# A first channel product with 15 multiplications for 18 on the last five token groups

## Chip, cores, metric

The kernel runs on one core of one Trainium2 chip. The metric is the device time of the program in microseconds (us). The profile's span runs from the first to the last instruction; the time is a little longer than the span.

## What is computed

A delta-rule attention over 4 batches, 8 heads, 768 tokens and a head size of 48, in which a 48x48 state per head is updated token by token, is followed by a mixer: a low-rank mixing over the tokens, and a channel block with a ReLU between two products.

```python
for t in range(S):                                   # S = 768
    y[:, :, t] = einsum('bhd,bhde->bhe', q[:, :, t], state)
    v_old = einsum('bhde,bhd->bhe', state, kt)       # kt: normalised key
    state = state + bt * einsum('bhd,bhe->bhde', kt, vt - v_old)
x = y.transpose(0, 2, 1, 3).reshape(B, S, 384)
h = x.transpose(0, 2, 1) @ U @ V                     # rank 32
u = x + h.transpose(0, 2, 1)
out = u + maximum(u @ w_ch1, 0) @ w_ch2              # 384 -> 1536 -> 384
```

All of it is float32.

## The kernel before

**Units and batches.** Attention goes in eight units n (batch b = n // 2, half of the sequence n % 2). A unit is loaded into one of two SBUF areas, `slots[n % 2]`, so that unit n + 2 is loaded only when unit n's recurrence no longer needs its slot. Its steps are: transpositions and products of keys and queries (`turn`, `products`: L671, L698), a triangular substitution on VectorE (`blocks`: L774, L783, L789, L796), the joining of its blocks (`joins`: L879, L882, then after a copy L887 the products L897, L900), two preparing products (`prepare`: L1000, L1011), and then six steps of the recurrence (`recur`: L1049 computes `b`, L1062 subtracts it on VectorE, L1077 and L1089 update the state, L964 and L978 give the outputs).

**Token groups.** The mixer works on twelve groups of 256 tokens (b, i), three to a batch. `front` mixes the tokens (L1378 once per batch, L1398, the addition L1407) and transposes the result into `ut` (L1426, L1429). `channels` is the first channel product: six steps e, each a pair of output tiles of 128, each tile three matmuls of 256 columns (the contraction of 384 is three tiles of 128), and `relu` (L1452) follows. The pair can be done as full-array matmuls (L1487) or in quarters of 64x64 (L432), which spares a change of array mode beside attention's quarter matmuls. `narrow` is the second channel product, in seven half-size products for eight (a Strassen-like scheme over halves of contraction, tokens and outputs): seven times six matmuls of 192 columns (L1602), with sums of activations from `add_up` (L1514) and `last_sum` (L1521). `gather` (L1527) adds the results to X on VectorE, and SP stores.

**The last batch.** For the three groups of batch 3 the first product is already done another way: `first_of_last` runs `quick(f)` for six f over all 768 tokens, in eleven matmuls of 384 columns (L1282) for twelve. Its sums of weights (L1242, L1250) and of tokens (L1266) are made on VectorE, and partial results go through ScalarE copies (L1300, L1304, L1309) and VectorE additions from PSUM (L1291).

```python
mm(px, w1_of(f, 0), u(0, 0), start=True, stop=True)
mm(pz, n1, t1, start=True, stop=True)
mm(py, w1_of(f, 1), u(1, 0), start=True)
mm(py, w1_of(f, 2), u(2, 0), stop=True)
...
mm(px, w1_of(f + HF, 1), t4)
mm(px, w1_of(f + HF, 2), t5, stop=True)
```

**What sets the order.** The instruction streams are written by a planner inside the kernel's own Python. Each step is a generator that yields `need(...)` (events that must have been emitted) or `op(engine, cost, mode, take, give)`. `run` picks, among the steps that could start next, the one with the lowest place, using planned costs in us, and then emits its instructions. A table `PLACES` gives most steps a place by name. PSUM has eight banks; the planner hands them out as four pairs (`pair`) for attention and fronts, and as single banks (`mix`) for the channel products. `reserve` takes banks 6 and 7 from the pairs for `mix` when batch 0 is nearly through its recurrence.

Of the kernel before, what the change touches and what calls it, by code (L numbers as in the profile page):

```python
# [19 lines left out]
GT = 256  # L20
# [6 lines left out]
def kernel(  # L27
# [52 lines left out]
    BANK = dict(pair=[0, 2, 4, 6], mix=[6, 7])  # L80
# [9 lines left out]
    SWITCH, HOLD, STAY = 0.18, 0.18, 0.15  # L90
    LOT, FETCH = 256, 4.1
    SPAN, PHASE = 3.413, 2.0

# [49 lines left out]
    add_up b0 i0 31.18; add_up b0 i1 51.08; add_up b0 i2 92.4; add_up b1 i0 4.76; add_up b1 i1 120.37  # L143
    add_up b1 i2 37.32; add_up b2 i0 75.44; add_up b2 i1 84.89; add_up b2 i2 77.05; add_up b3 i0 118.73
    add_up b3 i1 13.96; add_up b3 i2 89.72; blocks n0 109.59; blocks n1 122.78; blocks n2 46.87; blocks n3 118.73
    blocks n4 113.47; blocks n5 111.09; blocks n6 106.05; blocks n7 118.23; both -17.1; channels b0 i0 e0 48.87
    channels b0 i0 e0 quad 1; channels b0 i0 e1 -24.59; channels b0 i0 e1 quad 1; channels b0 i0 e2 105.07
    channels b0 i0 e3 120.72; channels b0 i0 e4 93.87; channels b0 i0 e4 quad 1; channels b0 i0 e5 71.17
    channels b0 i0 e5 quad 1; channels b0 i1 e0 91.19; channels b0 i1 e1 29.66; channels b0 i1 e1 quad 1
    channels b0 i1 e2 105.84; channels b0 i1 e3 111.44; channels b0 i1 e4 29.68; channels b0 i1 e5 93.86  # L150
    channels b0 i1 e5 quad 1; channels b0 i2 e0 126.42; channels b0 i2 e1 -13.48; channels b0 i2 e1 quad 1
    channels b0 i2 e2 123.41; channels b0 i2 e2 quad 1; channels b0 i2 e3 110.59; channels b0 i2 e4 29
    channels b0 i2 e4 quad 1; channels b0 i2 e5 29; channels b0 i2 e5 quad 1; channels b1 i0 e0 121.9
    channels b1 i0 e1 45.62; channels b1 i0 e2 51.81; channels b1 i0 e3 119.36; channels b1 i0 e3 quad 1
    channels b1 i0 e4 91.86; channels b1 i0 e4 quad 1; channels b1 i0 e5 88.71; channels b1 i0 e5 quad 1
    channels b1 i1 e0 92.89; channels b1 i1 e0 quad 1; channels b1 i1 e1 0.3; channels b1 i1 e2 123.36
    channels b1 i1 e3 87.93; channels b1 i1 e3 quad 1; channels b1 i1 e4 93.42; channels b1 i1 e4 quad 1
    channels b1 i1 e5 2.19; channels b1 i2 e0 75.94; channels b1 i2 e0 quad 1; channels b1 i2 e1 50.31
    channels b1 i2 e2 89.43; channels b1 i2 e2 quad 1; channels b1 i2 e3 121.39; channels b1 i2 e4 35.38
    channels b1 i2 e4 quad 1; channels b1 i2 e5 37.37; channels b1 i2 e5 quad 1; channels b2 i0 e0 110.33  # L160
    channels b2 i0 e0 quad 1; channels b2 i0 e1 38.43; channels b2 i0 e1 quad 1; channels b2 i0 e2 103.35
    channels b2 i0 e3 106.45; channels b2 i0 e3 quad 1; channels b2 i0 e4 123.83; channels b2 i0 e5 74.54
    channels b2 i0 e5 quad 1; channels b2 i1 e0 54.8; channels b2 i1 e0 quad 1; channels b2 i1 e1 13.42
    channels b2 i1 e2 104.03; channels b2 i1 e2 quad 1; channels b2 i1 e3 20.9; channels b2 i1 e3 quad 1
    channels b2 i1 e4 63.86; channels b2 i1 e4 quad 1; channels b2 i1 e5 20.4; channels b2 i1 e5 quad 1
    channels b2 i2 e0 41.46; channels b2 i2 e0 quad 1; channels b2 i2 e1 106.94; channels b2 i2 e1 quad 1
    channels b2 i2 e2 87.46; channels b2 i2 e2 quad 1; channels b2 i2 e3 20.4; channels b2 i2 e3 quad 1
    channels b2 i2 e4 24.2; channels b2 i2 e4 quad 1; channels b2 i2 e5 36.8; channels b2 i2 e5 quad 1
    copies 112.79; cut 126.91; diagonals n0 h0 55.7; diagonals n0 h1 53.68; diagonals n1 h0 3.93
    diagonals n1 h1 92.39; diagonals n2 h0 104.44; diagonals n2 h1 11.15; diagonals n3 h0 61.76  # L170
    diagonals n3 h1 33.65; diagonals n4 h0 47.84; diagonals n4 h1 106.43; diagonals n5 h0 1.02
    diagonals n5 h1 21.33; diagonals n6 h0 109.11; diagonals n6 h1 116.22; diagonals n7 h0 93.85
    diagonals n7 h1 75.29; first 110.09; first_of_last 49.99; front b0 i0 108.02; front b0 i0 quad 1
    front b0 i1 84.31; front b0 i2 91.39; front b0 i2 quad 1; front b1 i0 -10.61; front b1 i1 112.1
    front b1 i2 110.61; front b1 i2 quad 1; front b2 i0 63.6; front b2 i0 quad 1; front b2 i1 7.31
    front b2 i2 122.28; front b3 i0 105.93; front b3 i1 20.22; front b3 i2 109.1; gather b0 i0 h0 c0 -8.96
    gather b0 i0 h0 c1 -24.09; gather b0 i0 h1 c0 118.73; gather b0 i0 h1 c1 120.73; gather b0 i1 h0 c0 111.61
    gather b0 i1 h0 c1 94.36; gather b0 i1 h1 c0 118.74; gather b0 i1 h1 c1 94.39; gather b0 i2 h0 c0 30.48
    gather b0 i2 h0 c1 107.43; gather b0 i2 h1 c0 111.47; gather b0 i2 h1 c1 111.47; gather b1 i0 h0 c0 6.76
    gather b1 i0 h0 c1 111.08; gather b1 i0 h1 c0 110.6; gather b1 i0 h1 c1 111.1; gather b1 i1 h0 c0 122.88  # L180
    gather b1 i1 h0 c1 0.79; gather b1 i1 h1 c0 94.35; gather b1 i1 h1 c1 123.23; gather b1 i2 h0 c0 89.9
    gather b1 i2 h0 c1 121.66; gather b1 i2 h1 c0 1.2; gather b1 i2 h1 c1 108.09; gather b2 i0 h0 c0 118.24
    gather b2 i0 h0 c1 30.64; gather b2 i0 h1 c0 116.23; gather b2 i0 h1 c1 87.96; gather b2 i1 h0 c0 124.29
    gather b2 i1 h0 c1 109.6; gather b2 i1 h1 c0 117.94; gather b2 i1 h1 c1 29.2; gather b2 i2 h0 c0 21.73
    gather b2 i2 h0 c1 -8.77; gather b2 i2 h1 c0 30.5; gather b2 i2 h1 c1 113.04; gather b3 i0 h0 c0 -15.09
    gather b3 i0 h0 c1 61.92; gather b3 i0 h1 c0 14.46; gather b3 i0 h1 c1 91.38; gather b3 i1 h0 c0 -17.58
    gather b3 i1 h0 c1 118.32; gather b3 i1 h1 c0 11.47; gather b3 i1 h1 c1 15.47; gather b3 i2 h0 c0 90.44
    gather b3 i2 h0 c1 -10.43; gather b3 i2 h1 c0 -5.75; gather b3 i2 h1 c1 18.02; grams n0 i0 34.54
    grams n0 i1 3.69; grams n1 i0 -9.32; grams n1 i1 11.14; grams n2 i0 30.14; grams n2 i1 108.59; grams n3 i0 -2.69
    grams n3 i1 141.92; grams n4 i0 47.78; grams n4 i1 8.96; grams n5 i0 70.76; grams n5 i1 37.82; grams n6 i0 31.98  # L190
    grams n6 i1 9.07; grams n7 i0 111.04; grams n7 i1 60.31; joins n0 h0 27.2; joins n0 h1 55.69; joins n1 h0 3.19
    joins n1 h1 66.38; joins n2 h0 57.15; joins n2 h1 91.87; joins n3 h0 92.39; joins n3 h1 34.88; joins n4 h0 92.36
    joins n4 h1 105.93; joins n5 h0 94.89; joins n5 h1 21.39; joins n6 h0 -5.16; joins n6 h1 1.19; joins n7 h0 66.85
    joins n7 h1 104.02; last_sum b0 i0 110.92; last_sum b0 i1 116.73; last_sum b0 i2 103.44; last_sum b1 i0 -18.95
    last_sum b1 i1 -19.07; last_sum b1 i2 38.32; last_sum b2 i0 116.24; last_sum b2 i1 85.38; last_sum b2 i2 19.73
    last_sum b3 i0 109.31; last_sum b3 i1 -17.59; last_sum b3 i2 109.9; load n0 namek halves(0,) -16.25
    load n0 namek halves(1,) 28.17; load n0 nameq halves(0,) 4.52; load n0 nameq halves(1,) 67.79
    load n0 namev halves(0,) 127.05; load n0 namev halves(1,) 113.04; load n0 namez halves(0,) 5.44
    load n0 namez halves(1,) 99.93; load n1 namek halves(0,) 5.43; load n1 namek halves(1,) 60.81
    load n1 nameq halves(0,) -16.24; load n1 nameq halves(1,) 118.91; load n1 namev halves(0,) 47.34  # L200
    load n1 namev halves(1,) 49.87; load n1 namez halves(0,) 64.38; load n1 namez halves(1,) -10.34
    load n2 namek halves(0, 1) 21.89; load n2 nameq halves(0, 1) 22.39; load n2 namev halves(0, 1) 148.73
    load n2 namez halves(0, 1) -23.39; load n3 namek halves(0, 1) 70.26; load n3 nameq halves(0, 1) 40.96
    load n3 namev halves(0, 1) 63.6; load n3 namez halves(0, 1) 38.96; load n4 namek halves(0, 1) 94.39
    load n4 nameq halves(0, 1) 109.61; load n4 namev halves(0, 1) 45.72; load n4 namez halves(0, 1) 92.39
    load n5 namek halves(0, 1) 123.32; load n5 nameq halves(0, 1) 10.48; load n5 namev halves(0, 1) 78.69
    load n5 namez halves(0, 1) 10.98; load n6 namek halves(0, 1) 95.9; load n6 nameq halves(0, 1) 93.9
# [1473 lines left out]
```

## Time and profile before

| | before |
|---|---|
| time, median of 3 runs | 613.3 us (612.89 to 614.26) |
| profiled execution: time | 611.88 us |
| profiled execution: span | 610.2 us |
| mean granted clock of TensorE | 0.941 |
| TensorE (PE) busy | 571.3 us, 94% |
| VectorE (DVE) busy | 417.4 us, 68% |
| ScalarE (ACT) busy | 237.1 us, 39% |

Busy is the time in which at least one instruction of the engine runs. PE is the matmuls and PEld the weight loads that go ahead of them. A line of the grouped view names the source line, the engine, the operation, the tiles written and read, the number of records, their busy time and the mean length of one. In the timeline, records of one kind that follow one another are merged: start, length from the first start to the last end, and count.

### The profile page before, as it was taken

The page shows a single profiled execution, that of the slowest core. Times are in us where ns is not written, and L with a number is a line of the kernel's source. Part 1 is how long each engine was busy: PE and PEld are TensorE (multiplying, and loading weights), DVE is VectorE, ACT ScalarE, POOL GpSimd, SP SyncE. Part 2 cuts the span into 40 slices and gives each one's busy share as a digit, 9 for nine tenths or more (in the row PEclk, how much of TensorE's full clock was granted, in tenths as well). Part 3 has the DMA queues.
Part 4 walks back from the last instruction along what each step waited for, and adds up shares of the span by engine and source line. Part 5 has one row for each costly group of instructions (what it writes and reads, how often), then busy time and mean ns, then how long its engine had stood idle before and what let it go on. Part 6 is the DMA issues. An engine that isn't in the chain of part 4 may idle for free.

```text
span 610.2 us, 25422 instructions
## 1 busy us (share of the span) xinstructions
PE 571.3 (94%) x11502; PEld 497.0 (81%) x11502; DVE 417.4 (68%) x1000; ACT 237.1 (39%) x478; POOL 98.4 (16%) x169
## 2 busy tenths in 40 slices
PE   4788886699999999999999999999999999999997
PEld 4677876578888988988989987988989878656997
DVE  4999897898998528898887388869852124332542
ACT  2756654445522552246225522373152231344000
POOL 9141051520004110411032104300010000000000
PEclk9976556799999999999999999999999999999999
DMA  9731677921004320620050025300000000000000
GB/s 140 127 81 56 209 177 152 219 46 56 3 28 70 51 49 3 99 67 3 15 98 17 22 48 91 63 17 4 16 14 2 30 3 1 26 1 0 19 34 27
DMA packets 63852, 33.39 MB, mean 55 GB/s; under 512 B 50816, under 2 KB 61824, under 8 KB 63744
## 3 DMA queue, kind: packets, MB, share of 16 engines
q1 hardware_dynamic: 56800, 23.21, 18.4%
q0 software_dynamic: 5344, 8.27, 6.6%
q8 instruction: 90, 1.47, 1.0%
q10 hardware_dynamic: 1600, 0.30, 0.3%
q14 instruction: 18, 0.15, 0.1%
HBM read 27.03 MB, written 4.72 MB: 52 GB/s over the span
## 4 chain that ended last, share of the span: by engine, by line
PE 82%; DVE 10%; ACT 3%; issue 3%; DMA 1%; ACTq 0%; DVEq 0%
PE P L1602 26%; PE P L1487 18%; PE P L432 8%; PE P L1282 7%; PE P L698 3%; PE P L671 2%; PE P L1049 2%; PE P L978 2%; PE P L1011 2%; PE P L1000 2%; PE P L964 2%; PE P L1077 1%; DVE xt L789 1%; DVE prod L783 1%; PE P L853 1%
## 5 line engine op out<-in xcount | busy, mean ns | idle before, releaser
L1487 PE MATMUL P<-ut,w_sb 128*128 128x256 f32 x480 | 111.4, 385 | 0.4
L1487 PEld LDWEIGHTS P<-ut,w_sb 128*128 128x128 f32 x480 | 88.9, 190 | 12.9 <-ACT hs L1452 1.1
L1602 PE MATMUL P<-w_sb,hs 128*128 128x192 f32 x492 | 87.2, 331 | 0.1
L1602 PEld LDWEIGHTS P<-w_sb,hs 128*128 128x128 f32 x492 | 79.5, 190 | 2.7 <-ACT hs L1452 0.8
L1527 DVE TENSOR_TENSOR X<-X,P 128x192 f32<-128x192 f32 x84 | 29.5, 351 | 60.9 <-PE P L1602 59.3
L789 DVE TENSOR_TENSOR xt<-xt,prod 128x112 f32<-128x112 f32 (+21 forms) x200 | 64.6, 323 | 6.9
L783 DVE TENSOR_TENSOR prod<-gs,xt 128x112 f32<-128x112 f32 (+21 forms) x200 | 64.0, 320 | 4.6
L1452 ACT ACTIVATE hs<-P 128x512 f32<-128x512 f32 x54 | 32.3, 598 | 86.9 <-PE P L1487 66.0
L1602 PE MATMUL P<-w_sb,S 128*128 128x192 f32 x288 | 49.7, 328 | 0.0
L1602 PEld LDWEIGHTS P<-w_sb,S 128*128 128x128 f32 x288 | 46.7, 190 | 0.4 <-issue 0.3
L432 PE MATMUL P<-ut,w_sb 64*64 64x256 f32 x672 | 45.1, 383 | 1.8 <-ACT ut L1429 0.9
L948 ACT COPY X<-P 64x192 f32<-64x192 f32 x96 | 30.0, 312 | 38.1 <-PE P L978 29.7
L671 PE MATMUL P<-ident,slot 128*128 128x128 f32 x180 | 29.5, 315 | 11.0 <-DMA slot<-in_k_dram 9.4
L918 ACT COPY slot<-zz 32x384 f32<-32x384 f32 x64 | 32.4, 508 | 13.6 <-DVE zz L796 8.1
L555 POOL DMA_DIRECT2D slot<-in_k_dram x44 | 29.0, 667 | 44.1 <-PE P L1077 44.0
L671 PEld LDWEIGHTS P<-ident,slot 128*128 128x128 f32 x180 | 24.4, 163 | 13.3 <-issue 9.8
L555 POOL DMA_DIRECT2D slot<-in_q_dram x32 | 21.0, 665 | 84.0 <-DVE wide L1242 33.7
L698 PE MATMUL P<-slot 48*64 48x64 f32 x1536 | 32.1, 236 | 2.5 <-ACT slot L685 1.9
L1282 PE MATMUL P<-slot,w_sb 128*128 128x384 f32 x96 | 33.3, 486 | 0.0
L698 PEld LDWEIGHTS P<-slot 48*64 48x64 f32 x1536 | 29.0, 149 | 5.3 <-ACT slot L685 2.6
L555 POOL DMA_DIRECT2D slot<-in_v_dram x32 | 21.2, 669 | 70.7 <-PE P L671 63.0
L685 ACT COPY slot<-P 128x768 f32<-128x768 f32 x30 | 23.6, 797 | 22.8 <-PE P L671 17.5
(152 smaller groups left out, 978.5 us busy)
## 6 DMA issues: line engine op xcount, KB each, us to landing
out_dram<-X SPq DMA_DIRECT2D x22, 192.0 KB, 1.9
X<-in_moe_w_ch_dram SPq DMA_DIRECT2D x10, 384.0 KB, 4.2
wide<-in_moe_w_ch_dram SPq DMA_DIRECT2D x10, 384.0 KB, 4.3
slot<-in_k_dram SPq DMA_DIRECT2D x48, 72.0 KB, 5.0
slot<-in_k_dram POOLq DMA_DIRECT2D x44, 72.0 KB, 5.1
slot<-in_q_dram SPq DMA_DIRECT2D x32, 72.0 KB, 5.0
slot<-in_q_dram POOLq DMA_DIRECT2D x32, 72.0 KB, 5.5
slot<-in_v_dram SPq DMA_DIRECT2D x32, 72.0 KB, 3.0
```

The source lines that it names most:

```text
L432: nc.tensor.matmul(to[half(g)], w[half(r), half(g)], x[half(r)], start=start, stop=stop, skip_group_check=True,)
L555: queue.dma_start(out=t[half(1 - g if name == "z" else g), :, to, 0:D], in_=src[b, 4 * g + s, hf * UC * L : (hf + 1) * UC * L, :].rearrang ...
L671: nc.tensor.transpose(p_t[:, c // 3, c % 3], t[:, c, 2 * j : 2 * j + 2].rearrange("p s d -> p (s d)"), ident,)
L698: nc.tensor.matmul(p_g[half(g ^ (par * i)), par, c], kq[rows, c, j, 0, half(g)], kq[rows, c, j, i, half(g)], start=True, stop=True,)
L783: nc.vector.tensor_tensor(out=prod, in0=gb[:, :, j : j + 1, j + 1 :].to_broadcast([128, split, m, w]), in1=xb[:, :, 0:m, j : j + 1].to_bro ...
L789: nc.vector.tensor_tensor(out=xb[:, :, 0:m, j + 1 :], in0=xb[:, :, 0:m, j + 1 :], in1=prod, op=ALU.subtract,)
L918: nc.scalar.copy(pg[quarter(i), :, at, :, a : a + BK], cut(zc, h)[quarter(i)].rearrange("p r (c j) t -> p r c j t", j=2),)
L948: nc.scalar.copy(x[half(c % 2), c // 2, 4 * D * g : 4 * D * (g + 1)].rearrange("p (j r d) -> p r j d", r=2, d=D), states(p_y)[half(g)],)
L1282: nc.tensor.matmul(to, w, t, start=start, stop=stop, skip_group_check=True)
L1452: nc.scalar.activation(hs[:, fs[0] : fs[1] + 1 : fs[1] - fs[0]], p_f, ACTF.Relu)
L1487: nc.tensor.matmul(p_f[:, x], w(x, t), ut[:, t], start=(t == 0), stop=(t == KT - 1))
L1602: nc.tensor.matmul(to, of[0], of[1], start=of[2], stop=of[3], skip_group_check=True)
```

## The change

The first product of the last five groups, (2, 1), (2, 2), (3, 0), (3, 1) and (3, 2), is done in fifteen products for eighteen. The outputs are cut in thirds (four tiles of 128), the contraction in thirds (one tile of 128), and a group's tokens in halves (128). Each of the fifteen products is a sum of weight blocks times a sum of token blocks: four matmuls of 128 columns into one PSUM bank. The products are arranged in five chains. Within a chain each product is accumulated onto the bank's running sum, and between two products the bank is read: ScalarE copies it to the activations or VectorE adds or subtracts it there (`drain`), sixteen times for a group, and a ReLU pass follows. Fourteen sums of weight blocks are made once, in `slots[0]`, and eleven sums of token blocks for each group. Activations and sums of every second of the five groups lie in `slots[1]`. The chains use four PSUM banks (0 to 3), which `reserve` takes from the pairs when batch 3 has computed its last `b` and its last outputs. `quick`, `first_of_last` and their sums go; batch 3's groups become ordinary groups of 256 tokens.

Together with it the pairs of output tiles are put together otherwise (`PAIRS`), each weight slice is converted by a step of its own, many planned costs of the planner are set anew (a few are shown), and the table `PLACES` is new throughout. In the diff, cut to its core and with `CHAINS` set in fewer lines, a product of a chain is given as its weight block, its token block and, for each output that the bank is read into, that output, the sign, and how many terms it has had before.

```diff
-    BANK = dict(pair=[0, 2, 4, 6], mix=[6, 7])
+    BANK = dict(pair=[0, 2, 4, 6], mix=[6, 7, 0, 1, 2, 3])
...
-    SWITCH, HOLD, STAY = 0.18, 0.18, 0.15
+    SWITCH, HOLD, STAY = 0.11, 0.18, 0.15
+    LAP = 0.085
...
-    PAIRS = ((0, 1), (2, 6), (7, 8), (3, 4), (5, 9), (10, 11))
+    PAIRS = ((0, 1), (6, 7), (2, 8), (3, 9), (4, 5), (10, 11))
...
-        for i in range(len(slices)):
+        def convert(i, last):
...
-            yield need(("wide", i))
+            yield need(("wide", i), ("weights", last))
...
+    LAST, EARLY = B - 1, 7
+    W_SUMS = (
+        (6, 1, 7, 1), (8, 1, 9, -1), (3, 1, 10, 1), (5, 1, 11, -1), (1, 1, 4, -1), (12, -1, 13, -1),
+        (0, -1, 10, -1), (3, -1, 9, 1), (3, 1, 6, -1), (4, 1, 12, -1), (2, -1, 14, -1), (13, -1, 16, -1),
+        (2, 1, 15, 1), (0, 1, 9, -1),
+    )
+    T_SUMS = (
+        (1, 1, 5, 1), (2, 1, 4, 1), (3, 1, 7, 1), (0, 1, 6, 1), (2, -1, 3, -1), (5, -1, 8, -1),
+        (1, 1, 3, -1), (6, 1, 7, 1), (0, -1, 2, 1), (0, -1, 1, -1), (4, 1, 9, 1),
+    )
+    CHAINS = (
+        ((0, 0, ((0, 1, 0),)), (15, 9, ((1, -1, 1),)), (22, 6, ((5, -1, 1),)),
+         (16, 13, ((3, -1, 3),)), (11, 16, ((2, 1, 2),)), (17, 14, ((4, 1, 0),))),
+        ((1, 3, ((1, 1, 0),)), (14, 8, ((3, 1, 1),)), (18, 10, ((2, -1, 1),)), (19, 4, ((0, -1, 1),))),
+        ((20, 7, ((2, 1, 0),)), (12, 11, ((3, -1, 2),))),
+        ((10, 15, ((3, 1, 0), (5, 1, 0))), (21, 5, ((1, 1, 2),))),
+        ((7, 12, ((5, -1, 2),)),),
+    )
+    CHAIN_BANKS, TERMS = (2, 3, 4, 5, 4), (2, 3, 3, 4, 1, 3)
+    def ordinal(b, i):
+        return NG * b + i - EARLY
...
     def weight_sums():
-        yield need(("weights", W2 + 5), ("narrow", 1, 0))
...
+        yield need(("weights", W2 - 1), *freed(N - 2))
+        for z, (a, s, c, t) in enumerate(W_SUMS):
+            yield op("dve", dve(512), port=True)
+            sum_of(w_block(9 + z), w_block(a), s, w_block(c), t)
+            emitted(("weight sum", 9 + z), 0.1)
...
+    def token_sums(b, i):
+        yield need(
+            ("front", b, i), *[("wide", *before(*before(b, i)))] * (ordinal(b, i) > 1),
+            *freed(N - 1 if ordinal(b, i) % 2 else N - 2),
+        )
+        for z, (a, s, c, t) in enumerate(T_SUMS):
+            yield op("dve", dve(128), port=True)
+            sum_of(token(b, i, 6 + z), token(b, i, a), s, token(b, i, c), t)
+            emitted(("token sum", b, i, 6 + z), 0.1)
...
+    def products_of(b, i, e):
+        y = CHAIN_BANKS[e]
+        yield need(
+            ("front", b, i), ("mixing", 0), *[("chain", b, i, x) for x in range(e) if CHAIN_BANKS[x] == y],
+            *[("chain", *before(b, i), x) for x in range(len(CHAINS)) if CHAIN_BANKS[x] == y and ordinal(b, i)],
+        )
+        bank = mixed(y).rearrange("p (q n) -> p q n", q=4)
+        def drain(c, outs, final):
+            yield need(cleared(b, i), *freed(N - 1) * (ordinal(b, i) % 2))
+            for z, (o, s, k) in enumerate(outs):
...
+                if k == 0:
+                    yield op("act", act(512), rush=True, give=give)
+                    nc.scalar.activation(
+                        to, p, ACTF.Relu if TERMS[o] == 1 else ACTF.Copy, scale=float(s)
+                    )
+                else:
+                    yield need(("held", b, i, o, k - 1))
+                    yield op("dve", dve(512), rush=True, give=give)
+                    nc.vector.tensor_tensor(
+                        out=to, in0=to, in1=p, op=ALU.add if s > 0 else ALU.subtract
+                    )
...
+        for c, (w, t, outs) in enumerate(CHAINS[e]):
+            yield need(
+                *[("drained", b, i, e, c - 1)] * (c > 0 and len(CHAINS[e][c - 1][2]) > 0),
+                *[("weight sum", w)] * (w > 8), *[("token sum", b, i, t)] * (t > 5),
+            )
+            yield op("pe", 0.875, "F", take=None if c else ("mix", y), words=16)
+            for q in range(4):
+                nc.tensor.matmul(
+                    bank[:, q], w_block(w)[:, q // 2, 128 * (q % 2) : 128 * (q % 2) + 128],
+                    token(b, i, t), start=c == 0 and q == 0, stop=True,
+                    skip_group_check=True,
+                )
...
-    def quick(f):
...
-    def first_of_last():
...
     def reserve():
...
+        yield need(("b", LAST, NC - 1))
+        yield op("pe", 0.0, take=("pair", 0))
+        free["mix"].update({2: state["now"], 3: state["now"]})
+        emitted(("mixing", 0))
+        yield need(*[("x", LAST, c) for c in range(NC)])
+        yield op("pe", 0.0, take=("pair", 1))
+        free["mix"].update({4: state["now"], 5: state["now"]})
...
     def wide(b, i):
-        yield need(("front", b, i), ("half" if b == LAST else "narrow", *before(b, i), *[3] * (b == LAST)))
+        yield need(("front", b, i), cleared(b, i), *freed(N - 1) * (ordinal(b, i) > 0 and ordinal(b, i) % 2))
...
-        if b == LAST:
+        if ordinal(b, i) >= 0:
             for f0 in range(0, HF, 3):
                 begin(add_up(f0, ()), 4)
...
         else:
             for e in range(len(PAIRS)):
                 begin(channels(e), 95)
...
-        begin(first_of_last(), 94)
...
+                if ordinal(b, i) >= 0:
+                    begin(first_of(b, i), 94)
```

## Prediction

> **What bounds the kernel now.** I read the page first, then the stage table (busy time of each engine in each stretch), then the timeline of TensorE for the price of one product, then the waits at the end. On the page, the slices tell the shape: the granted clock is low in the first fifth and full from about 122 us on, and from there PE is at nine tenths or more to the last slice.
>
> ```profile
> PE 571.3 (94%) x11502; PEld 497.0 (81%) x11502; DVE 417.4 (68%) x1000; ACT 237.1 (39%) x478; POOL 98.4 (16%) x169
> PE   4788886699999999999999999999999999999997
> DVE  4999897898998528898887388869852124332542
> PEclk9976556799999999999999999999999999999999
> ```
>
> The stage table says the same in us, cut at three events: the clock's rise, the end of the last substitution on VectorE (its transposition L796 starts at 445.9) and the start of the last batch's mixing (L1378 at 500.7).
>
> ```profile
> 0.00:122.00 122.00, 91.53 (x2706) 83.17 (x2710) 102.47 (x244) 64.82 (x125) 43.29 (x76) 0.71 0.72 145
> 122.00:446.00 324.00, 320.82 (x7100) 282.95 (x7093) 259.37 (x641) 129.38 (x260) 53.51 (x89) 1.00 0.20 42
> 446.00:500.00 54.00, 53.03 (x1116) 46.01 (x1118) 15.02 (x31) 19.99 (x47) 1.65 (x4) 1.00 0.03 10
> 500.00:610.20 110.20, 105.93 (x598) 84.86 (x590) 40.59 (x86) 22.92 (x48) 0.00 (x0) 1.00 0.04 15
> ```
>
> The columns are length, PE, PEld, DVE, ACT and POOL busy, clock, DMA. From 122 us on PE is busy 479.8 of 488.2 us: the sum of its work sets the end, and a us of work removed there is a us of time as long as other work stands ready. VectorE has 324 - 259.4 = 64.6 us idle between 122 and 446, and is three quarters idle from 446 to 500, while attention still runs.
>
> **The price of a product.** A full-array float32 matmul leaves two records (504 second-product matmuls in twelve groups: 480 as 960 records, 24 in quarters); a transposition leaves one. In the timeline, of a run of n records the first starts at the first number, the second is its length; less one record's own length, over n - 1, that gives the spacing.
>
> ```profile
> 450.69 9.33 PE L1487 MATMUL P<-ut,w_sb 128*128 128x256 f32 x42
> 517.87 4.07 PE L1602 MATMUL P<-w_sb,hs 128*128 128x192 f32 x24
> 528.87 2.74 PE L1282 MATMUL P<-slot,w_sb 128*128 128x384 f32 x8
> 506.08 0.82 PE L1426 MATMUL P<-ident,X 128*128 128x128 f32 x6
> ```
>
> With record lengths of 385, 331, 486 and 276 ns (the groups by line): 256 columns 0.218 us, 192 columns 0.163, 384 columns 0.322, and the transposition, 128 columns, 0.109. The spacing is proportional to the columns within 3%.
>
> **What goes.** The first product of the last five groups, two groups of batch 2 and three of batch 3. Batch 2's two are 36 matmuls of 256 columns each: 2 x 72 x 0.218 = 31.4 us; five of their twelve steps run in quarters (L432, 24 records start to start 1.34 us, so 2.68 a step for 2.59 in full), 0.5 more. Batch 3 is `quick`, eleven matmuls of 384 columns for each of six f: 132 records x 0.322 = 42.5 us. Together 74.4 us of PE.
>
> **What comes.** Five groups x fifteen products x four matmuls of 128 columns: 600 records. No such record is in this trace: the row that has its columns and its weights (128x128) is the transposition, at 0.109, and the line through the three wide rows comes out at 0.108. Bounds: 0.109 below; above, 0.163, the narrowest full-array float32 product seen, if something in a pair other than the columns sets it. I take 0.109, since two rows agree: 65.4 us. PE gains **9.0 us**.
>
> The one difference from the transposition is the weight load: 190 ns for a product, 141 for a transposition (same rows, PEld). At 0.163 spacing loads of 190 ns already overlap (PEld reads 79.5 us for 492 of them, 0.162 each), so 190 is a latency in the main; whether its rate holds at 0.109 no row shows.
>
> The Trainium skill (TensorE: Matmul & The Clock Gate, Back-to-back issue gap) speaks against the change here: in pairs of load and matmul the spacing is set by both, about 81 ns at 128 columns where an isolated matmul needs 56. Adding those 25 ns to each record, an estimate from that page, would make the products 80.4 us and the sum a loss of 6.0. The same page's LDWEIGHTS section puts a 128-column load at 107 ns, by which the gain stays; this trace's transpositions at 109 ns bear out the second.
>
> VectorE gets, for each of the five groups, ten additions of 512 columns from PSUM (between L1291, 384 columns 554 ns, and L1407, 768 columns 950 ns: 0.69 us, 6.9), eleven token sums of 128 columns (L1242, 0.29 us, 3.2), and keeps `add_up` (6 x 0.55), `last_sum` (0.95) and seven gathers (2.5): about 17.8 us with the front's addition, under 13.1 + 13.7 = 26.8 us of PE for first and second product. ScalarE gets eleven passes of 512 columns (L1452, 598 ns): 6.6. Neither is the bound; if their cover went, it would be the 1.9 us of a link (product 0.87, addition 0.69, hand-overs 0.3) that PE waits, but four banks run chains side by side, and the longest, six links, needs 11.4 us of the 26.8. The fourteen weight sums (9.7 us; `weight_sums` now costs 7) lie after unit 6's recurrence on a VectorE that is idle then. The end of the program (last matmul 606.9, then addition and store, 3.3 us) is the same.
>
> **What is moved.** This decides. The products of all five groups use PSUM banks 0 to 3, which `reserve` takes from attention only when batch 3 has computed its last `b` (the last run of L1049; banks 2 and 3 after its last outputs, L978); before, batch 2's groups ran among batch 3's recurrence.
>
> ```profile
> 498.04 0.40 PE L1049 MATMUL P<-s,slot 48*64 48x48 f32 x16
> 498.26 0.41 PE L978 MATMUL P<-z,slot 64*64 64x48 f32 x16
> 499.25 1.49 PE L432 MATMUL P<-ut,w_sb 64*64 64x256 f32 x24
> ```
>
> So the release came at 498.3. After it PE now has 65.4 of first products, 5 x 84 x 0.163 = 68.3 of second, 5.1 of batch 3's fronts, and the 3.3: 142 us. For a span of 610.2 - 9.0 = 601.2 the release must come by 459, 39 us earlier; every us later is a us of PE idle, for no other work is left. Where it can come from: after the last substitution, L879 runs at 449.8 and its continuation L897 only at 467.8, with 17 us of first and second products put between, though the copy that it waits for (L887) takes 0.32 us; and the last unit's five recurrence steps take 21.5 us (L1062 at 477.1 to 498.6), 4.3 each, where batch 0's run at 2.9 (82.0, 84.9, 87.8): 7 us. That is 24. The other 15 must come from VectorE's 64.6 idle us before 446, and from the 5.2 us of old weight sums that leave that stretch (L1242, 300 to 320 us). VectorE would have to be busy (259.4 - 5.2) of 309 us there, 82%, for 80% now. PE's own work is only reordered: what yields to attention fills later, batch 1's groups under batch 3. I take all 39 as found; from none found, the span would be 498.3 + 142 = 640.
>
> The order everywhere else is new too (a new table of places, other pairs of output tiles, weight conversions that can be placed one by one). Its price no row gives. Bounds: in the first 122 us PE idles 30 us, its longest gaps 5.2 and 3.5 us; I take 0, and one such gap either way for the range.
>
> **Sum.** The profiled execution took 611.88 us around its span of 610.2, 1.4 below the median of 613.3. It would be 602.9; on the median, 604.3. I say 604.
>
> **Rivals.** (a) *The banks come free late.* For it: attention is a chain over two slots and VectorE has filled 80% of 122 to 446 already. Against: the 24 us of plain delay. If only those 24 are found, the release is 15 us late: a span of 616, 619 us. It is a loss from the point where less than 30 of the 39 are found. (b) *Weight loads bind.* The row against is the transposition; the row for it is the 190 to 141 ns. If those 49 ns add to the spacing, 600 x 0.158 = 94.8 us: slower by 20, 634 us. By the Trainium skill's 81 ns it would be 619. (c) *The new order gains in the first stage.* If the two long gaps (8.7 us) go there, 595 to 596; nothing in the profile says that they must. That the products would not shrink as stated is no rival: fifteen for eighteen is counted in the chains.
>
> **Chances.** Forecast 0.62 (its own range 599 to 609), (a) 0.18, (b) 0.06, (c) 0.14. About 0.2%, 1.2 us, is what a measurement of this kernel can tell from none. Faster: forecast and (c), less 0.02 of the forecast's edge, 0.74; same 0.04 (that edge and a part of (a)); slower 0.22. The range from 595 to 618 leaves out (b), half of (a) and the low end of (c), 0.19.
>
> **What would show it.** Right: 128-column float32 records spaced 0.109 us, 600 of them; the last L1049-like run near 459 and PE over 95% after it; VectorE below seven tenths in the tail. Wrong: spacing of 0.13 or more (b); or a gap of PE, several us long, ahead of the first fifteen-product group (a), the clock falling in it; or long waits of PE on the additions in PSUM, which would mean that the chains are too few.

## The result and the profile after

| | before | changed |
|---|---|---|
| median | 613.8 us (4 runs, 612.9 to 617.9) | 607.1 us (4 runs, 606.4 to 608.5) |
| ratio, 95% interval | | 0.988 (0.983 to 0.993) |
| profiled execution: time, span | 611.88, 610.2 us | 606.39, 604.6 us |
| release of banks 0 and 1 (last L1049, now L1079) | 498.2 us | 454.8 us |

The change is faster by 6.7 us, and by 7.9 in a second set of runs (614.0 and 606.1, ratio 0.988, 0.985 to 0.990). I had said 604.

The page after, same rows: busy time of each engine, then the slices.

```profile
PE 571.3 (94%) x12072; PEld 515.9 (85%) x12072; DVE 450.9 (75%) x1074; ACT 242.1 (40%) x481; POOL 97.7 (16%) x169
PE   5888987799999999999999999999999999999997
DVE  4999999998988898598634899899744656367442
PEclk9999566699999999999999999999999999999999
```

The stage table, cut at the clock's rise, the last substitution (L826 starts at 417.0) and the release. Columns: length, PE, PEld, DVE, ACT, POOL busy, clock, DMA.

```profile
0.00:122.00 122.00, 96.06 (x2723) 87.53 (x2727) 107.33 (x251) 64.90 (x127) 42.66 (x76) 0.80 0.71 151
122.00:417.00 295.00, 291.02 (x7181) 252.04 (x7176) 241.03 (x600) 123.52 (x255) 53.42 (x89) 1.00 0.20 42
417.00:455.00 38.00, 37.91 (x1029) 33.44 (x1024) 24.34 (x53) 16.59 (x37) 1.65 (x4) 1.00 0.03 9
455.00:604.60 149.60, 146.26 (x1174) 142.85 (x1166) 78.23 (x171) 37.09 (x63) 0.00 (x0) 1.00 0.04 16
```

VectorE is now at 52% in the last stretch; in the last stretch of before (from 500 us on) it was at 37%. PE is idle for 4.1 us between 122 us and the release, and not at all from the release to its last matmul at 601.3 us; the 3.3 us behind that are the end of the program. The weight loads (PEld) have become 95% of the last stretch; in the last stretch of before they were 77%. The timeline of PE around the release and in the first fifteen-product group:

```profile
454.83 0.39 PE L1008 MATMUL P<-z,slot 64*64 64x48 f32 x12
455.11 1.16 PE L461 MATMUL P<-w_sb,hs 64*64 64x192 f32 x23
456.00 0.49 PE L1008 MATMUL P<-z,slot 64*64 64x48 f32 x16
...
464.57 1.06 PE L1402 MATMUL P<-slot,w_sb 128*128 128x128 f32 x8
465.46 1.06 PE L1402 MATMUL P<-slot 128*128 128x128 f32 x8
466.36 1.06 PE L1402 MATMUL P<-ut,slot 128*128 128x128 f32 x8
467.30 1.16 PE L1402 MATMUL P<-slot 128*128 128x128 f32 x8
```

L1402 is the fifteen products, eight records for each. A product of 1.06 us length has records (1.06 - 0.275) / 7 = 0.112 us apart. The fourth row, 1.16, has one spacing of 0.21 in it, and 0.94 us instead of 0.90 lie between its start and the start before. Summed over all 600 records, from each start to the next on PE, the products take 69.7 us.

Where the 5.6 us of span come from, by the same sums (from each record's start to the next, from 122 us on):

| | before | changed |
|---|---|---|
| first product, plain, full and quarters | 146.4 | 115.4 |
| first product, `quick` / fifteen products | 42.6 | 69.7 |
| second product | 170.5 | 170.2 |
| everything else | 125.2 | 124.0 |
| sum | 484.7 | 479.3 |

The first stretch, from PE's first record to 122 us, gives 0.4 (117.0 and 116.6). So 3.9 of the 5.6 us are the first products'. The other 1.7 are spread over attention, fronts and second products, and no experiment takes them apart: "everything else" differed by 2.5 us between two executions of one and the same kernel (126.0 and 123.5, the version with 0.5 us planned, below).

### The profile page after: what moved, and what is told of

Same layout as the page of the kernel before. It is cut to its first block, busy times and chain, and to the rows that moved or that the text cites. A ratio compares the mean times of both kernels' runs of the same rounds, so it can differ in the third digit from the quotient of the medians.

```text
span 604.6 us, 26613 instructions
## 1 busy us (share of the span) xinstructions
PE 571.3 (94%) x12072; PEld 515.9 (85%) x12072; DVE 450.9 (75%) x1074; ACT 242.1 (40%) x481; POOL 97.7 (16%) x169
## 3 DMA queue, kind: packets, MB, share of 16 engines
q1 hardware_dynamic: 56800, 23.21, 17.6%
## 4 chain that ended last, share of the span: by engine, by line
PE 80%; DVE 12%; issue 3%; ACT 3%; DMA 1%; ACTq 0%; DVEq 0%
PE P L1667 23%; PE P L1552 14%; PE P L1402 12%; PE P L461 10%; PE P L728 4%; PE P L701 2%; PE P L1079 2%; DVE prod L813 2%; DVE xt L819 2%; PE P L1030 2%; PE P L994 1%; PE P L1107 1%; PE P L1008 1%; PE P L1041 1%; PE P L1458 1%
## 5 line engine op out<-in xcount | busy, mean ns | idle before, releaser
L1552 PE MATMUL P<-ut,w_sb 128*128 128x256 f32 x360 | 84.9, 387 | 0.3 <-DVE X L1592 0.2
L1552 PEld LDWEIGHTS P<-ut,w_sb 128*128 128x128 f32 x360 | 66.2, 190 | 10.0 <-issue 0.6
L819 DVE TENSOR_TENSOR xt<-xt,prod 128x112 f32<-128x112 f32 (+21 forms) x200 | 64.6, 323 | 6.9
L1517 ACT ACTIVATE hs<-P 128x512 f32<-128x512 f32 x42 | 25.1, 597 | 61.4 <-PE P L1552 43.3
L461 PE MATMUL P<-ut,w_sb 64*64 64x256 f32 x576 | 39.0, 385 | 1.9 <-ACT hs L1517 1.4
L728 PE MATMUL P<-slot 48*64 48x64 f32 x1536 | 34.4, 250 | 3.5 <-ACT slot L715 2.8
L728 PEld LDWEIGHTS P<-slot 48*64 48x64 f32 x1536 | 31.1, 161 | 7.4 <-ACT slot L715 4.9
L1384 DVE TENSOR_TENSOR hs<-hs,P 128x512 f32<-128x512 f32 x30 | 20.2, 687 | 21.3 <-PE P L1402 12.0
L1667 PE MATMUL P<-w_sb,S 128*128 128x192 f32 x192 | 33.0, 328 | 0.0
L1402 PE MATMUL P<-slot 128*128 128x128 f32 x240 | 31.5, 278 | 0.0
L1667 PEld LDWEIGHTS P<-w_sb,S 128*128 128x128 f32 x192 | 31.2, 190 | 0.2
```

The costliest lines, as they stand in the source:

```text
L461: nc.tensor.matmul(to[half(g)], w[half(r), half(g)], x[half(r)], start=start, stop=stop, skip_group_check=True,)
L728: nc.tensor.matmul(p_g[half(g ^ (par * i)), par, c], kq[rows, c, j, 0, half(g)], kq[rows, c, j, i, half(g)], start=True, stop=True,)
L819: nc.vector.tensor_tensor(out=xb[:, :, 0:m, j + 1 :], in0=xb[:, :, 0:m, j + 1 :], in1=prod, op=ALU.subtract,)
L1402: nc.tensor.matmul(bank[:, q], w_block(w)[:, q // 2, 128 * (q % 2) : 128 * (q % 2) + 128], token(b, i, t), start=c == 0 and q == 0, stop=True,
L1552: nc.tensor.matmul(p_f[:, x], w(x, t), ut[:, t], start=(t == 0), stop=(t == KT - 1))
L1667: nc.tensor.matmul(to, of[0], of[1], start=of[2], stop=of[3], skip_group_check=True)
```

## The experiments

The theory was the prediction's: PE's sum sets the end, a group in fifteen products is cheaper than a plain one, and the order has only to bring the release forward. The main rivals were that the gain is the new order's, and that the weight loads bind.

**No group in fifteen products.**

```diff
-    LAST, EARLY = B - 1, 7
+    LAST, EARLY = B - 1, 12
```

> EARLY = 12: no group is done in fifteen products; the last five are done in the plain eighteen, as the first seven, under the changed order and its table. Theory (the sum of PE's work sets the end): a plain group costs 6 steps x 2.75 us = 16.5 us (115.4 us for the 42 steps that the changed kernel has), fifteen products 13.9 us (69.7 us for five), so five groups cost 12.7 us more: about 619 to 620 us, ratio to before 1.01. Some of it can come back, since the plain groups need not wait for the banks: not below 614. Rival (the gain is the new order, the products are worth nothing): 607 us, within 1.5.

Measured: 620.7 us, ratio to before 1.010 (1.007 to 1.014), 13.6 over the changed kernel where 12.7 were expected. The attention is nearly where it was in the changed kernel (the last `b` at 455.8 for 454.8), so the order is kept. By itself the order gains nothing; it is slower than before by what `quick` had saved: five plain groups in place of two plain ones and `quick`, 3 x 16.5 - 42.6 = 6.9 us, and it is 6.8 slower.

**Three groups.**

```diff
-    LAST, EARLY = B - 1, 7
+    LAST, EARLY = B - 1, 9
```

> EARLY = 9: only the three groups of batch 3 in fifteen products, the two of batch 2 plain. Theory (PE's sum): 2 x 2.5 = 5.1 us more, 612 us. Rival (order alone): 607. Third (the release of the banks costs PE time even in the changed kernel): under 607, since less then stands behind the release.

Measured: 611.7 us, ratio 0.996 (0.994 to 0.999): the theory's number. With the release at 454 us and the first fifteen-product group at 482.8, the release bound nothing here, and still it is slower than with five groups. So in the changed kernel the release costs no PE time that this can show, which agrees with its trace, where PE has no gap behind the release.

**Six groups.**

```diff
-    LAST, EARLY = B - 1, 7
+    LAST, EARLY = B - 1, 6
```

> EARLY = 6: a sixth group, (2, 0), is done in fifteen products. It then stands behind the release of the banks, like the five. Theory with the release as a second bound: PE has 2.5 us less to do, but the first product (13.9) and the second (14.1) of this group no longer fill the stretch before the release near 455 us, and PE idles there for up to 28 us less what the order can pull forward: 615 to 632 us, with gaps of PE ahead of the release. Rival (the release is no bound, only PE's sum): 604.5 us.

Measured: 632.1 us, ratio 1.030 (1.025 to 1.035), at the top of what the second bound allowed; the rival's 604.5 is out. The stage table, of an execution of 635.9 us, the longest of four:

```profile
300.00:400.00 100.00, 98.41 (x2289) 85.95 (x2291) 70.87 (x175) 43.30 (x85) 23.21 (x40) 1.00 0.26 52
400.00:425.00 25.00, 17.55 (x527) 15.66 (x516) 22.33 (x66) 4.71 (x14) 0.00 (x0) 0.92 0.06 19
425.00:452.00 27.00, 19.33 (x752) 17.41 (x752) 14.99 (x34) 13.05 (x30) 1.65 (x4) 0.56 0.01 4
452.00:634.20 182.20, 177.31 (x1408) 171.90 (x1408) 92.40 (x199) 42.45 (x72) 0.00 (x0) 0.98 0.04 14
```

Up to 400 us PE is full. From 400 to 452 it idles 15.1 us while VectorE (22.3 of 25 us) finishes the last substitution, and the granted clock falls to 0.56, so that the rest of the attention costs more too: a record of the outputs (L1008) takes 290 ns between 425 and 452 us, where it takes 218 between 417 and 455 in the changed kernel. The release comes at 449.9 us and the first group starts at 452.2; behind it stand six groups. This is rival (a) of the prediction, made by one more group behind the release.

**Without the table of places.** The string `PLACES` is emptied in both kernels.

> The changed kernel with an empty table of places: every step has its default place. The other run does the same to the kernel before. Theory (the gain is the products', the table only has to bring the release of the banks forward): here PE idles ahead of the first fifteen-product group, since the defaults bring nothing forward, and this kernel is the slower of the two, by 5 us or more. Rival (the change carries its gain whatever the order): faster than the kernel before without its table by 6 to 7 us.

> The kernel before with an empty table of places, to stand beside the run above. Theory and rival as there; its own time is expected above 613, by an amount that nothing so far bounds (620 to 680).

Measured: the changed kernel 682.1 us, the kernel before 632.3, ratios to before 1.111 (1.107 to 1.115) and 1.031 (1.026 to 1.035). The slices, first the changed kernel's PE and clock, then those of the kernel before:

```profile
PE   5587967899999999999999989996167999999998
PEclk9857586799999999999999959997555899999999
```

```profile
PE   5588866699999999999999999999999999999997
PEclk9857578689999999999999999999999999999999
```

The change, in the default order, loses 50 us. The release comes at 525 us, about as late as the last `b` of the other kernel (520), and between 122 us and the release PE idles 38.7 us, 15.8 of them in one gap, with the clock down to a half in the slices. The kernel before idles 7.5 us up to its last `b`; its groups of batch 2 need no release. The difference in idle time is 31 of the 50 us, and the rest was not taken apart. So much of what the table does for this change is to move the release, which is what the prediction's sum took as found.

**Half of the token columns.** The products of the last five groups stream 64 of 128 columns.

```diff
...
-                    bank[:, q], w_block(w)[:, q // 2, 128 * (q % 2) : 128 * (q % 2) + 128],
-                    token(b, i, t), start=c == 0 and q == 0, stop=True,
+                    bank[:, q, 0:64], w_block(w)[:, q // 2, 128 * (q % 2) : 128 * (q % 2) + 128],
+                    token(b, i, t)[:, 0:64], start=c == 0 and q == 0, stop=True,
```

> Each of the fifteen products streams 64 of its 128 token columns; the other half of the result is left out. (The clearing of PSUM at the start covers whole banks here and in the next run.) It asks what sets the 0.112 us between two records of 128 columns, where transpositions of the same size stand 0.109 apart. If the columns set it: 0.053 to 0.060 us between records, the products 32 to 36 us for 69.7, the time 575 to 590 us, with more waits on the reads of the banks. If the weight loads (128 columns each, unchanged here) set it: the spacing stays at 0.10 to 0.112 and the time at 603 to 608 us.

**Half of the weight columns.**

```diff
...
-                    bank[:, q], w_block(w)[:, q // 2, 128 * (q % 2) : 128 * (q % 2) + 128],
+                    bank[0:64, q], w_block(w)[:, q // 2, 128 * (q % 2) : 128 * (q % 2) + 64],
```

> Each product uses 64 of its 128 weight columns; half of the outputs of the last five groups is left out. Token columns stay 128. If the weight loads set the 0.112 us: the spacing falls to 0.109 or less (the columns' own 0.107 and a rest). If the columns and a fixed rest set it: 0.112 still, and the time stays at 606 to 608 us.

Measured, a single time each: 606.8 us with half the token columns, 612.8 with half the weights. Rows of the timeline, first with half the token columns:

```profile
489.73 1.63 PE L1667 MATMUL P<-w_sb,hs 128*128 128x192 f32 x9
491.20 1.00 PE L1402 MATMUL P<-slot,slot 128*128 128x64 f32 x8
493.92 1.06 PE L1402 MATMUL P<-slot,slot 128*128 128x64 f32 x8
496.77 1.06 PE L1402 MATMUL P<-slot 128*128 128x64 f32 x8
```

and with half the weight columns:

```profile
493.74 1.04 PE L1402 MATMUL P<-slot,w_sb 128*64 128x128 f32 x8
495.61 1.04 PE L1402 MATMUL P<-slot,slot 128*64 128x128 f32 x8
```

With 64 columns to stream instead of 128 a product is as long as before, records 0.112 us apart (the median of all 600). So not the columns but the weight loads set the 0.112. The second row shows the other side: it follows second products of 192 columns, 0.163 us apart, behind which the loads could go ahead. Its first spacing is 0.056 us (hence 1.00 for 1.06), and from the second on it is 0.112 again; seventeen first spacings in this trace are of 0.055 to 0.058 us, sixteen of them behind second products. So 0.112 is no fixed price of a record: one whose load is done can follow after 0.056. With 64 weight columns and 128 token columns the median falls to 0.109, as in transpositions. Together: the loads of 128 float32 columns follow one another at 0.112 us, a little slower than 128 columns stream (0.109).

That the second run is still slower in time lies elsewhere. Its spacings over 0.15 us are 65 instead of 33, its full-array second products take 144.2 us for 141.1, and everything else 126.8 for 124.0, of which run-to-run differences can be a part (2.5 us between two executions of the 0.5 version below). The trace marks short idle times of PEld ("issue", 0.2 us) where loads of 64 and of 128 columns alternate, but that was not tried by itself.

**Reads of the banks planned longer.**

```diff
-            emitted(("drained", b, i, e, c), 0.1)
+            emitted(("drained", b, i, e, c), 0.5)
```

> The planner counts 0.5 us instead of 0.1 from the end of a read of a bank to the next product of its chain, so that it puts other work there. In the changed kernel 33 of the 600 records are followed by a spacing of 0.16 us or more where the others have 0.112: 2.7 us. Theory (these are products that wait for the read of their bank, with the weight load behind the wait): most of them go, 605 us. Rival (the work that is put there only moves the wait): 607 or more.

Measured: 605.9 us, ratio 0.986 (0.982 to 0.990). Spacings over 0.15 us are 16 for 33, the products 68.6 us for 69.7: half of the waits went, not most. The same again, with the changed kernel beside it and two variants:

> The changed kernel once more, to stand beside the next three on the same chip: 607 us, within 1.5.

> late_drain once more (0.5 us planned from a read of a bank to the chain's next product): faster than the changed kernel by the 1.1 us that its products were shorter (68.6 for 69.7), if that is more than chance: 606 us. Rival: no difference, 607.

```diff
-            emitted(("drained", b, i, e, c), 0.1)
+            emitted(("drained", b, i, e, c), 0.9)
```

> 0.9 us planned for the same. Theory (spacings of 0.16 us and more are products that wait for a read): fewer than the 16 that 0.5 left, the products 67.5 to 68.5 us, 605.5. Rival (the chains become too few to fill PE and PE idles instead): PE's idle time after the release above 1 us, 607 or more.

```diff
-            emitted(("drained", b, i, e, c), 0.1)
+            emitted(("drained", b, i, e, c), 0.5)
...
-            yield op("pe", 0.875, "F", take=None if c else ("mix", y), words=16)
+            yield op("pe", 0.9, "F", take=None if c else ("mix", y), words=16)
```

> late_drain with a product planned at 0.9 us, as it was measured (eight records of 0.112), for 0.875. Theory: planned and real order of the reads meet better, 605 to 606 us. Rival: the planned price of a product doesn't matter for the order, as late_drain_2.

| | median | ratio to before, 95% | products | spacings over 0.15 us |
|---|---|---|---|---|
| changed, again | 606.1 us | 0.988 (0.985 to 0.990) | 69.7 us | 33 |
| 0.5 planned, again | 604.8 | 0.985 (0.982 to 0.987) | 68.6 | 16 |
| 0.9 planned | 606.8 | 0.988 (0.986 to 0.990) | 69.4 | 17 |
| 0.5, product at 0.9 | 607.6 | 0.989 (0.986 to 0.992) | 69.7 | 19 |

The 1.1 us is in both traces of the 0.5 version, and its median was 1.2 and 1.4 us below the changed kernel's in the two sets; the intervals overlap, so the time alone doesn't show it. It has the lowest median of all versions. The last two missed their expectation: 17 and 19 long spacings are fewer than the 33 of the changed kernel, but not fewer than the 16 of the 0.5 version, and each trace has one of 1.05 us. With 0.9 planned, PE idles there, and this row names what for:

```profile
537.43 1.06 PE L1402 MATMUL P<-slot 128*128 128x128 f32 x8
539.26 1.16 PE L1402 MATMUL P<-slot 128*128 128x128 f32 x8 [0.78 <-DVE hs L1384]
```

A product waits for VectorE's read of its bank (L1384). The changed kernel's trace says the same of its own long spacings. Of the 33, three (0.205 us) stand before a front's products and 30 between two records of the fifteen products. Of these 30, 29 lie directly before or behind the first record of a product that waited for a read of a bank (L1384, or L1378 on ScalarE), and this read had ended 0.05 to 0.11 us before that record. Such a wait also lays the product's first weight load open: elsewhere in a product a load starts about 0.11 us ahead of its matmul, here together with it (467.296 and 467.298 us). The cost at that place is 0.161 and then 0.213 us (from 467.14 and 467.30 on) where two spacings of 0.112 would be: 0.15 lost, the wait included.

## Why the prediction was right, and what was off

The direction, the mechanism and the range held; the size was 9.0 us for a measured 6.7 to 7.9. The total of what was moved came out partly by luck: its two halves were both miscounted, in opposite directions (below).

- **What goes** was forecast at 74.4. `quick` measured 42.6 (42.5 forecast). The plain steps cost 2.71 us each before (146.4 for 54), 32.5 for the twelve that went (31.9 forecast; the row I took, 0.218 a record, was a run without a wait in it). But the 42 that stay cost 2.75 in the new order, and these 0.04 took 1.5 us back, which the sum had not; why they cost more was not tried.
- **What comes** is the term that was mis-sized: 65.4 forecast, 69.7 measured, 0.116 us a record for 0.109. Of the 4.3 us, about 1.6 is the weight load, shown by the halved columns (the spacings without a wait are 0.1116 in the mean, 600 x 0.0026); 2.4 is the excess over 0.112 of the 30 long spacings between records of the products, which the trace shows as waits for reads, and of which the planned 0.5 took back 1.1; 0.3 is the three spacings before fronts. The prediction had said that four chains side by side would hide the reads; they hid most of them.
- **Rival (b)**, weight loads that bind, was right in kind and wrong by far in price: they bind at 0.112, not at 0.158. The 49 ns between loads of 190 and of 141 ns, from which it was priced, are not the rate: loads of 191 ns follow one another at 0.112, 3 ns over the transpositions' spacing. Of the two figures of the Trainium skill (TensorE: Matmul & The Clock Gate), the LDWEIGHTS section's, 107 ns for 128 columns by its formula, is near the measured 112. The 25 ns a record that the prediction had estimated from the section Back-to-back issue gap did not come: 0.112 for 0.109.
- **What is moved.** The release had to come by 459 us and came at 454.8; 39 us earlier was asked, 43 found. Of them 14.5 lie after the last substitution (52.3 us before, 37.8 now; I had counted 24) and 29 before it (15 counted). Of the 24, the delay between L879 and L897 gave 13.1 us (18.1 before, 5.0 now between L909 and L927), but the five recurrence steps only 1.2 of the 7 (21.5 before, 20.3 now). Ahead of the last substitution VectorE's idle time fell from 64.6 to 54.0 us, about as worked out (54.8); the surplus came from work that left the stretch, 259.4 us before and 241.0 now, of which the prediction had counted the 5.2 of old weight sums. So VectorE's share of 82% is as forecast, of a shorter stretch. PE after the release is busy 146.3 of 149.6 us, 98%. That this was the deciding step, with rival (a) as its other side, six groups and the empty table show: 25 and 75 us over the changed kernel, with PE idle ahead of the release in both.
- **VectorE's cover** held: an addition of 512 columns took 687 ns (0.69 forecast), and VectorE is at 52% in the tail, below the seven tenths.
- **Rival (c)**, a gain in the first stretch from the new order, did not come: 116.6 us for 117.0, and the two long gaps are still there (5.4 and 3.3 us for 5.2 and 3.5). The clock there differed from run to run of nearly the same program (0.64 with no group, 0.82 with three), while the last `b` stayed within 1.7 us (454.1 to 455.8). So PE's clock there hardly moves the end of attention; that VectorE sets it, busy 107 of those 122 us, is likely and was not tested.

## What to carry to other kernels

A scheme with fewer multiplications pays by the matmul only down to the width at which the weight load takes as long as the columns: here 128 columns, for with 64 the products took as long. Price it from the nearest row with the same weights, and then look for that row's load. When new work needs a resource that an older stage holds, count the work that is left to fill the time before the release and the work that stands behind it: here three groups left 4.6 us of five's gain unused, and six cost 25 (four were not tried). The order decides whether such a change pays at all: with default places it lost 50 us against the kernel before with default places.

## What the runs showed of the hardware

- Records of float32 products with 128x128 weights stood 0.112 us apart (median), whether 128 or 64 columns streamed; a record of 64 columns whose successor's load had gone ahead during wider products was followed after 0.056 (16 times). With 64 weight columns and 128 streamed it was 0.109, and in transpositions of 128x128, whose loads are 141 ns long for 190, 0.109.
- A product that waited for the read of its bank cost some 0.15 us in two spacings (0.161 and 0.213 for 0.112 each): its first weight load started with the matmul instead of 0.11 us ahead of it.
- With six groups PE was at seven tenths busy from 400 to 452 us. The granted clock was 0.92 in the first 25 us of it (17.6 busy) and 0.56 in the other 27 (19.3 busy); up to 400 us in the same run, at 98% busy, it was 1.00.
